# Retention and two mixtures of experts on one core: the front's work moved between engines

## The chip, the core and the metric

The kernel runs on one core of a Trainium2 chip. The metric is device time in microseconds (us). A core has a matrix engine (TensorE, PE in rows; its weight loads are PEld), VectorE (DVE), ScalarE (ACT), GpSimd (POOL) and SyncE (SP), which here only issues transfers. Each engine works through its own list of instructions in order and waits on semaphores for the others.

## The reference

All arithmetic is in 32-bit floats. With 2 sequences, 8 heads, 768 steps and head size 64:

```
state = gamma * state + k_t (x) v_t         per head, 64 x 64
y_t   = q_t . state / sqrt(64)              -> x, 1536 tokens x 512
logits = x @ w_gate  (8 experts)            expert = argmax, weight = softmax at it
each token goes to its expert, in order, up to capacity 384
h = relu(x @ w1[e]); y = h @ w2[e]          8 experts, hidden size 1024
out = sum over 4 domains of p_d * (relu(y @ u1[d]) @ u2[d])
```

## The kernel before

The program has a front (retention, routing, gathering the first expert's tokens) and then two long matrix stages, the 8 experts and the 4 domain experts. The change touches the front alone.

The front takes the 1536 tokens in 12 tiles of 128 steps (6 to a sequence) and is a software pipeline, written out by hand in the loop of line 458: `tc.manual_schedule()` keeps the written order on every engine. Round `it` works on several tiles at once:

- `st_v` (247): v of tile it+1 times a decay per head, on GpSimd, into vg.
- `st_S` (257): scores k.q of tile it for 8 heads, on TensorE, 64 rows by 128 columns at a time; then VectorE multiplies by the causal mask into sd.
- `st_I`, `st_U`, `st_O` (301, 278, 315): state times q, update of the state sum, and vg times sd, all for tile it-1 on TensorE. ScalarE copies the state out (st). The sixth tile of a sequence has no U, the first no I.
- `st_x` (327): the output of tile it-1 times a scale table gqs. ScalarE copies it out of the accumulation memory (PSUM) to ot, GpSimd multiplies into xT; for the last two tiles VectorE does both in one step.
- `x_pe` and `x_reduce` (355, 374), tile it-2: TensorE multiplies xT by iw, an identity beside the gate's weights, which turns the tile back and yields the logits. VectorE sums the logits, ScalarE copies the tokens to xk, and ScalarE's queue stores xk to memory.
- `x_dve` (393), tile it-2: eight small steps on VectorE to the one-hot expert choice ohs, the running count cum and ohk, the one-hot times the token's number.
- `r_pe` and `r_dve` (347, 420), tile it-3: a rank of each token in its expert from two small products, read back by VectorE, and compared with slot numbers (`slot_at`, at).
- `g_pe` (443), tile it-4: at times ohk sums up which token sits in which slot.

`braid` (451) emits two chains of VectorE step by step in turn. The kernel uses eight banks of PSUM: four rotate among scores, outputs, ranks and warm-up; four are held for the slots, the state, and X (x0 and x1).

SyncE issues loads in a fixed order: qk and kv of a tile (512 KB each), the tables gqs (256 KB each), iw and kc. Round `it` loads tile it+3. From round 6 on the first weights are loaded as well, and at the end of round 8 `split_w(0)` (131) splits one: a copy on ScalarE, then a subtraction on VectorE.

After the loop (500 to 581) the last tiles run out. `late` multiplies tokens of the last two tiles straight into the first expert's input T0x; `fetched` adds those that a GpSimd gather brought from memory. Line 950 is the first expert product.

Of the kernel before, what the change touches and what calls it, by code (L numbers as in the profile page):

```python
# [29 lines left out]
XW = KD * 136  # L30
# [5 lines left out]
DEPTH = 4  # L36
HT = 384
# [21 lines left out]
def tile_retention_moe_moe(ctx: ExitStack, tc, qkv, cst, gqt, a0, a1, a2, b1, b2, out, cap):  # L59
# [16 lines left out]
    banks = [f"bank{n}" for n in range(4)]  # L76
    held = ["slot", "u", "x0", "x1"]
    nbank = [0]

    def bank(name, tag=None):  # L80
        if tag is None:
            tag = banks[nbank[0] % len(banks)]
            nbank[0] += 1
        return ps[0].tile([P, 512], F32, tag=tag, name=name)

# [107 lines left out]
    with ExitStack() as actx:  # L193
# [7 lines left out]
        iw = pa.tile([P, KD, 136], F32, name="iw")  # L201
        zero = pa.tile([1, D], F32, name="zero")
# [7 lines left out]
        slot_ps = bank("slot_ps", "slot")[:, 0:SL // P * E1].rearrange(  # L210
# [21 lines left out]
        load_qk(1)  # L232
        load_gq(0)
        load_kv(1)
        nc.sync.dma_start(out=iw.rearrange("p a b -> p (a b)"), in_=cst[:, C_IW:C_U])
        load_qk(2)
        nc.sync.dma_start(out=kc, in_=cst[:, C_U:])
        load_gq(1)
        load_kv(2)
# [7 lines left out]
        def st_v(i):  # L247
            kv = kv_t.pop(i)
            vg = p2.tile([P, 8, HD], F32, tag="vg", name=f"vg{i}", bufs=3)
            nc.gpsimd.tensor_tensor(  # L250
                out=vg, in0=kv[:, 1].rearrange("p (h d) -> p h d", h=8),
                in1=gk[:, i % NCH].rearrange("p (h d) -> p h d", d=1).to_broadcast([P, 8, HD]),
                op=ALU.mult,
            )
            live[i] = {"vg": vg, "k": kv[:, 0]}

        def st_S(i):
            qk = qk_t.pop(i)
            sd = p2.tile([P, 2, 512], F32, tag="sd", name=f"sd{i}")
            live[i].update(sd=sd, q=qk[:, 0])  # L260
            bks = [bank(f"S{i}_{j}") for j in range(2)]
            for hp in range(4):
                cols = slice(hp * P, (hp + 1) * P)
                for j in range(2):
                    r = slice(64 * j, 64 * j + 64)
                    nc.tensor.matmul(
                        out=bks[j][:, cols], lhsT=qk[r, 1, cols], rhs=qk[r, 0, cols],
                        start=True, stop=True,
                    )
# [8 lines left out]
        def st_U(i):  # L278
# [3 lines left out]
            if c == 0:  # L282
                u_ps[0] = bank(f"U{i}", "u")
# [17 lines left out]
        def st_I(i):  # L301
            c = i % NCH
            live[i]["o"] = [bank(f"O{i}_{j}") for j in range(2)]
# [23 lines left out]
        def st_x(i):  # L327
# [4 lines left out]
            if i < NT - 2:  # L332
                ot = p2.tile([P, 512], F32, tag="ot", name=f"ot{i}")
                for j in range(2):
                    nc.scalar.copy(ot[:, 256 * j:256 * j + 256], bks[j][:, 0:256])
                nc.gpsimd.tensor_tensor(out=xT, in0=ot, in1=gqs[:, c], op=ALU.mult)
            else:
                for j in range(2):
                    cols = slice(256 * j, 256 * j + 256)
                    nc.vector.tensor_tensor(  # L340
                        out=xT[:, cols], in0=bks[j][:, 0:256], in1=gqs[:, c, cols], op=ALU.mult
                    )
# [4 lines left out]
        def r_pe(i):  # L347
            bk = bank(f"R{i}")
            nc.tensor.matmul(out=bk[:, 0:8], lhsT=onesb, rhs=cum[:, i], start=True, stop=False)
            nc.tensor.matmul(out=bk[:, 0:8], lhsT=ub, rhs=ohs[:, i], start=False, stop=True)  # L350
            rl[i] = bk[:, 0:8]

        xks = {}

        def x_pe(i, reduce=True):
            xT = live.pop(i)["xT"]
            xk = xks[i] = p2.tile([P, D], F32, tag="xk", name=f"xk{i}", bufs=3)
            part = p2.tile([P, 8], F32, tag="part", name=f"part{i}")
            if i == NT - 1:
                bks = [bank(f"X{i}_{g}") for g in range(2)]  # L360
            else:
                bks = [bank(f"X{i}_{g}", f"x{g}") for g in range(2)]
            for hp in range(KD):
                nc.tensor.matmul(
                    out=bks[hp // 2][:, (hp % 2) * 136:(hp % 2 + 1) * 136],
                    lhsT=xT[:, hp * P:(hp + 1) * P], rhs=iw[:, hp], start=True, stop=True,
                )
            xbs[i] = bks, part
# [3 lines left out]
        xbs = {}  # L372

        def x_reduce(i):
            bks, part = xbs.pop(i)
            xk = xks[i]
            for g in range(2):
                b3 = bks[g][:, 0:272].rearrange("p (q c) -> p q c", q=2)
                nc.vector.tensor_reduce(
                    out=part if g else lgs[:, i], in_=b3[:, :, P:136].rearrange("p q e -> p e q"),  # L380
                    axis=AX.X, op=ALU.add,
                )
                nc.scalar.copy(
                    xk.rearrange("p (b k c) -> p k b c", b=4, k=KD)[:, 2 * g:2 * g + 2],
                    b3[:, :, 0:P].rearrange("p q (b c) -> p q b c", b=4),
                )
            nc.scalar.dma_start(out=xd[1 + i * P:1 + (i + 1) * P], in_=xk)
            nc.vector.tensor_tensor_reduce(
                out=lgs[:, i], in0=lgs[:, i], in1=part, scale=1.0, scalar=-FMAX, op0=ALU.add,
                op1=ALU.max, accum_out=mxs[:, i],  # L390
            )
# [161 lines left out]
        for b in range(SL // P):  # L553
            fetched(b, range(2))
# [858 lines left out]
```

## Time and profile before

| | |
|---|---|
| median of 3 runs | 735.69 us (735.53 to 737.09) |
| profiled execution | 735.49 us |
| its span, first to last instruction | 733.7 us |
| granted TensorE clock | 0.999 |
| PE busy | 722.3 us (98%) |
| DVE, ACT, POOL busy | 473.5, 339.0, 202.5 us |

Times in rows count from the start of the span. A row of the timeline has its start, its duration, the engine, the line, the operation, what is written and read, and, in brackets, the idle time just before it with what ended it. Rows of one line that follow one another are merged, with their count. Each 32-bit product shows as two passes (16 for the 8 score products). A row of a stretch has the length, then busy time and instructions of PE, PEld, DVE, ACT and POOL, the granted clock, the share of the DMA engines and GB/s.

### The profile page before, as it was taken

How to read it: one execution, taken by the hardware profiler on the slowest of the kernel's cores; microseconds unless marked ns; L12 is line 12 of the kernel's file. 1: busy time of each engine (PE TensorE's matmuls, PEld its weight loads, DVE VectorE, ACT ScalarE, POOL GpSimd, SP SyncE). 2: the span in 40 equal slices, each digit the busy share in tenths (PEclk: the TensorE clock that was granted, in tenths of full speed). 3: DMA queues.
4: the chain of work that ended last, by engine and by line, in shares of the span. 5: the costliest groups of instructions: out<-in, count | busy, mean ns of one | idle time of the engine just before them, and what ended most of it. 6: DMA issues, size and time to landing. Idle time of an engine off the chain costs nothing.

```text
span 733.7 us, 11338 instructions
## 1 busy us (share of the span) xinstructions
PE 722.3 (98%) x4425; PEld 657.2 (90%) x4426; DVE 473.5 (65%) x777; ACT 339.0 (46%) x545; POOL 202.5 (28%) x193
## 2 busy tenths in 40 slices
PE   8998999999999999999999999999999999999997
PEld 6887999999999888999889998889998899988896
DVE  3888899898898835545743655763475454557334
ACT  2344767676656533334433445633344334444331
POOL 3653854443044012212323111223422121111103
PEclk9999999999999999999999999999999999999999
DMA  9984886687741211211122122122222212112102
GB/s 331 414 338 138 287 320 220 228 281 245 230 144 34 89 55 59 86 58 58 61 91 78 38 77 87 59 85 88 87 72 71 92 53 86 59 58 79 37 1 86
DMA packets 28026, 92.83 MB, mean 127 GB/s; under 512 B 4097, under 2 KB 4369, under 8 KB 27970
## 3 DMA queue, kind: packets, MB, share of 16 engines
q1 hardware_dynamic: 23042, 81.79, 32.2%
q0 software_dynamic: 3056, 7.05, 2.8%
q10 hardware_dynamic: 1872, 3.24, 1.2%
q8 instruction: 35, 0.57, 0.3%
q14 instruction: 21, 0.17, 0.1%
HBM read 85.72 MB, written 6.34 MB: 125 GB/s over the span
## 4 chain that ended last, share of the span: by engine, by line
PE 88%; DVE 1%; POOL 1%; ACT 0%; issue 0%; POOLq 0%; ACTq 0%
PE o L1212 35%; PE a L1056 17%; PE m L950 15%; PE b L1056 9%; PE m L953 7%; PE bb L1056 5%; POOL out_dram L1224 1%; PE ab L1056 0%; DVE x L855 0%; DVE X L868 0%; ACT X L864 0%; DVE c L1149 0%; POOLq L1409 0%; ACT c L1087 0%; PE T L768 0%
## 5 line engine op out<-in xcount | busy, mean ns | idle before, releaser
L1212 PE MATMUL o<-w,g_c 128*128 128x512 f32 x1152 | 267.4, 390 | 0.0
L1212 PEld LDWEIGHTS o<-w,g_c 128*128 128x128 f32 x1152 | 215.9, 188 | 43.7
L142 DVE TENSOR_TENSOR w<-raw,w 128x1024 fp32r<-128x1024 f32 x128 | 158.4, 1247 | 13.9 <-ACT w L141 13.6
L1056 PE MATMUL a<-X,w 128*128 128x384 f32 x720 | 145.2, 336 | 0.0
L157 POOL TENSOR_TENSOR t<-raw 128x512 f32<-128x512 f32 x28 | 38.8, 1386 | 349.6 <-DMA raw<-b 302.2
L1091 DVE TENSOR_TENSOR c<-b,c 128x384 f32<-128x384 f32 x30 | 16.7, 558 | 181.1 <-PE b L1056 181.1
L141 ACT CAST w<-raw 128x1024 fp32r<-128x1024 f32 x128 | 132.1, 1047 | 2.5 <-DMA raw<-a 1.1
L1056 PEld LDWEIGHTS a<-X,w 128*128 128x128 f32 x720 | 127.5, 188 | 2.6 <-DVE c L1091 0.3
L1087 ACT COPY c<-a 128x384 f32<-128x384 f32 x60 | 28.8, 479 | 196.3 <-PE a L1056 196.3
L950 PE MATMUL m<-xet,w 128*128 128x448 f32 x256 | 80.8, 375 | 0.8 <-PEq L635 0.8
L1072 ACT ACTIVATE g_c<-c 128x384 fp32r<-128x384 f32 x96 | 50.4, 526 | 66.0 <-DVE c L1091 64.7
L950 PE MATMUL m<-h,w 128*128 128x448 f32 x256 | 80.8, 375 | 0.0
L1056 PE MATMUL b<-X,w 128*128 128x384 f32 x360 | 72.1, 334 | 0.0
L953 PE MATMUL m<-h,w 128*128 128x224 f32 x256 | 67.5, 264 | 0.0
L953 PE MATMUL m<-xet,w 128*128 128x224 f32 x256 | 67.5, 264 | 0.0
L624 POOL DMA_INDIRECT xe<-xd,gidx x42 | 53.7, 1278 | 47.3 <-DVE xT L752 35.7
L1056 PEld LDWEIGHTS b<-X,w 128*128 128x128 f32 x360 | 63.5, 188 | 0.0
L1076 DVE SCALAR_TENSOR_TENSOR g_c<-c,g_c 128x384 fp32r<-128x384 f32 x96 | 52.9, 552 | 3.9
L950 PEld LDWEIGHTS m<-xet,w 128*128 128x128 f32 x256 | 48.0, 187 | 4.6 <-PEq L635 1.0
L950 PEld LDWEIGHTS m<-h,w 128*128 128x128 f32 x256 | 48.0, 187 | 3.7
L953 PEld LDWEIGHTS m<-xet,w 128*128 128x128 f32 x256 | 48.9, 191 | 0.0
L953 PEld LDWEIGHTS m<-h,w 128*128 128x128 f32 x256 | 48.9, 191 | 0.0
(158 smaller groups left out, 766.7 us busy)
## 6 DMA issues: line engine op xcount, KB each, us to landing
raw<-a SPq DMA_DIRECT2D x64, 512.0 KB, 4.9
raw<-b SPq DMA_DIRECT2D x64, 512.0 KB, 3.5
qk<-qkv SPq DMA_DIRECT2D x12, 512.0 KB, 8.3
kv<-qkv SPq DMA_DIRECT2D x12, 512.0 KB, 8.1
xd<-xk ACTq DMA_DIRECT2D x12, 256.0 KB, 6.2
gqs<-gqt SPq DMA_DIRECT2D x6, 256.0 KB, 7.5
xe<-xd,gidx POOLq DMA_INDIRECT x44, 4.9
iw<-cst SPq DMA_DIRECT2D x1, 272.0 KB
```

Source lines behind the costliest of these rows:

```text
L141: nc.scalar.copy(w[:, 0], r)
L142: nc.vector.tensor_tensor(out=w[:, 1], in0=r, in1=w[:, 0].bitcast(F32), op=ALU.subtract)
L157: eng.tensor_tensor(out=c[:, 0:2], in0=b[:, 2:4], in1=b[:, 1:3], op=sub)
L624: nc.gpsimd.indirect_dma_start(out=t[:, b], out_offset=None, in_=xq, in_offset=bass.IndirectOffsetOnAxis(ap=gidx[:, b, e:e + 1], axis=0),)
L950: nc.tensor.matmul(out=b2, lhsT=w[0], rhs=x, start=first, stop=last, skip_group_check=True)
L953: nc.tensor.matmul(out=b2[:, 0], lhsT=w[1], rhs=x[:, 0], start=False, stop=last, skip_group_check=True)
L1056: nc.tensor.matmul(out=bk[:, 0:HT], lhsT=w[:, sw, k], rhs=x[:, sx, k], start=(first and m == 0), stop=(m == len(steps) - 1), skip_group_ch ...
L1072: nc.scalar.activation(out=h2[:, 0], in_=src, func=AF.Relu)
L1076: nc.vector.scalar_tensor_tensor(out=h2[:, 1], in0=src, scalar=0.0, in1=h2[:, 0].bitcast(F32), op0=ALU.max, op1=ALU.subtract,)
L1087: nc.scalar.copy(t, bk[:, 0:HT])
L1091: nc.vector.tensor_tensor(out=t, in0=bk[:, 0:HT], in1=t, op=ALU.add)
L1212: nc.tensor.matmul(out=bk, lhsT=h2[:, sh, cols], rhs=w[:, sw, k], start=(q == 0 and m == 0 and (n, t) not in begun), stop=(m == 2), skip_g ...
```

## The change

- v (from tile 2 on) is made on ScalarE, one instruction for each of the 8 heads.
- The output product is always made by VectorE straight from PSUM; the copy to ot and GpSimd's product go.
- A score product is cut into two of 64 rows by 64 columns, and from round 4 on the scores of tile it are issued at the start of round it.
- PSUM: one bank pair each for scores (s2), outputs (o2) and X (x), besides slot and u. The rank product goes into X's second bank, ahead of X. One reduction takes all four logit parts, one copy makes xk, and the maximum is a plain reduction.
- ohk moves to ScalarE; the slot numbers get a 16-bit copy, rnk16, for the comparison.
- iw is loaded as one identity and the gate's weights (ig, 80 KB instead of 272 KB) and spread by ScalarE in round 1.
- Loads: kv of tiles 1 and 2 go ahead of the tables.
- The end runs in another order.

```
-        load_gq(0)
         load_kv(1)
-        nc.sync.dma_start(out=iw..., in_=cst[:, C_IW:C_U])
+        load_gq(0)
         load_qk(2)
+        load_kv(2)
+        nc.sync.dma_start(out=ig, in_=cst[:, C_IW:C_U])
         nc.sync.dma_start(out=kc, in_=cst[:, C_U:])
         load_gq(1)
-        load_kv(2)
...
 def st_v(i):
+            if i < 2:
                 nc.gpsimd.tensor_tensor(out=vg, in0=v, in1=..., op=ALU.mult)
+            else:
+                for h in range(8):
+                    nc.scalar.activation(
+                        out=vg[:, h], in_=v[:, h], func=AF.Copy, scale=gk[:, i % NCH, h:h + 1]
+                    )
...
 def st_S(i):
-            bks = [bank(f"S{i}_{j}") for j in range(2)]
+            s2 = two("s2", f"S{i}")
+            bks = [s2[:, j] for j in range(2)]
             for hp in range(4):
-                for j in range(2):
+                for m in range(4):
+                    o, j = 64 * (m >> 1), m & 1
                     nc.tensor.matmul(
-                        out=bks[j][:, cols], lhsT=qk[r, 1, cols], rhs=qk[r, 0, cols],
+                        out=bks[j][o:o + 64, cols],
+                        lhsT=qk[r, 1, hp * P + o:hp * P + o + 64], rhs=qk[r, 0, cols],
...
 def st_x(i):
-            if i < NT - 2:
-                    nc.scalar.copy(ot[:, 256 * j:256 * j + 256], bks[j][:, 0:256])
-                nc.gpsimd.tensor_tensor(out=xT, in0=ot, in1=gqs[:, c], op=ALU.mult)
-            else:
                 for j in range(2):
                     nc.vector.tensor_tensor(out=xT[:, cols], in0=bks[j][:, 0:256], ...)
...
+        def x_pe(i, rank=None, reduce=True):
+            b2 = xbs[i] = two("s2" if i == NT - 1 else "x", f"X{i}")
+            if rank is not None:
+                r_pe(rank, b2[:, 1, 448:456])
...
 def x_reduce(i):
+            nc.vector.tensor_reduce(out=lgs[:, i], in_=b3[:, :, P:136]..., axis=AX.X, op=ALU.add)
+            nc.scalar.copy(xk..., b3[:, :, 0:P]...)
             nc.scalar.dma_start(out=xd[1 + i * P:1 + (i + 1) * P], in_=xk)
+            nc.vector.tensor_reduce(out=mxs[:, i], in_=lgs[:, i], axis=AX.X, op=ALU.max)
...
         for it in range(NT):
+            if it >= EARLY_S:        # 4
+                st_S(it)
             ...
-            st_S(it)
+            if it < EARLY_S:
+                st_S(it)
...
         st_I(NT - 1)
-        x_pe(NT - 2)
-        r_pe(NT - 3)
         st_O(NT - 1)
-        braid(r_dve(NT - 3))
-        g_pe(NT - 4)
-        g_pe(NT - 3)
         st_x(NT - 1)
+        x_pe(NT - 2, NE - 1, False)
+        g_pe(NE - 2)
+        braid(r_dve(NE - 1))
+        g_pe(NE - 1)
         (slot numbers out, gather issued)
+        x_reduce(NT - 2)
+        x_pe(NT - 1, None, False)
         braid(x_dve(NT - 2))
-        x_pe(NT - 1, False)
-        r_pe(NT - 2)
-        braid(r_dve(NT - 2))
+        r_pe(NT - 2, one("u", "R10")[:, 0:8])
         x_reduce(NT - 1)
-        braid(x_dve(NT - 1))
+        braid(r_dve(NT - 2), x_dve(NT - 1))
```

## Rows read from the trace of the kernel before

**Rows 1.** Busy time by stretches: the rounds, the end, the expert stages.
```profile
20.00:55.00 35.00, 34.58 (x569) 30.44 (x569) 29.81 (x115) 12.96 (x38) 20.23 (x22) 1.00 0.93 374
55.00:68.40 13.40, 11.11 (x112) 9.66 (x111) 10.73 (x59) 4.26 (x10) 2.12 (x2) 1.00 0.41 134
68.40:733.70 665.30, 659.42 (x3528) 604.43 (x3528) 424.07 (x583) 316.67 (x484) 173.44 (x158) 1.00 0.32 107
```

**Rows 2.** Timeline of the weight loads, one round.
```profile
48.96 0.97 PEld L266 LDWEIGHTS S<-qk 64*128 64x128 f32 x16 [0.17 <-issue]
50.05 0.99 PEld L364 LDWEIGHTS X<-iw,xT 128*128 128x128 f32 x8
...
51.26 0.43 PEld L309 LDWEIGHTS O<-qk,st 64*64 64x64 f32 x16
51.86 0.55 PEld L290 LDWEIGHTS U<-vg,kv 128*64 128x64 f32 x16 [0.17 <-issue]
52.32 0.91 PEld L321 LDWEIGHTS O<-sd,vg 128*64 128x64 f32 x16
53.40 0.30 PEld L266 LDWEIGHTS S<-qk 64*128 64x128 f32 x4 [0.17 <-issue]
```

**Rows 3.** The same timeline: X of tiles 1, 2 and 9, and one wait.
```profile
18.79 0.99 PEld L364 LDWEIGHTS X<-iw,xT 128*128 128x128 f32 x8
...
23.32 0.99 PEld L364 LDWEIGHTS X<-iw,xT 128*128 128x128 f32 x8
...
35.30 0.96 PEld L266 LDWEIGHTS S<-qk 64*128 64x128 f32 x14 [0.54 <-DVE ranks L424]
...
54.49 0.99 PEld L364 LDWEIGHTS X<-iw,xT 128*128 128x128 f32 x8
```

**Rows 4.** Timeline of GpSimd: v of tiles 3 and 4.
```profile
19.59 1.04 POOL L250 TENSOR_TENSOR vg<-kv,cdec 128x512 f32<-128x512 f32 x1 [2.26 <-PE X L364]
...
22.93 1.04 POOL L250 TENSOR_TENSOR vg<-kv,cdec 128x512 f32<-128x512 f32 x1 [1.06 <-DMA kv<-qkv]
```

**Rows 5.** ScalarE: first xk (timeline); groups (count, busy us, mean ns, idle before).
```profile
17.53 0.65 ACT L383 COPY xk<-X 128x256 f32<-128x256 f32 x2 [4.21 <-DVE lgs L379]
...
L383 ACT COPY xk<-X 128x256 f32<-128x256 f32 x24 | 7.8, 375 | 21.2 <-DVE lgs L379 18.1 <-DVE part L379 3.1
L141 ACT CAST w<-raw 128x1024 fp32r<-128x1024 f32 x6 | 6.2, 1048 | 1.3 <-DMA kv<-qkv 0.9 <-ACT xk L383 0.4
```

**Rows 6.** DMA issues: size of iw.
```profile
iw<-cst SPq DMA_DIRECT2D x1, 272.0 KB
```

**Rows 7.** Timeline of VectorE in the last round.
```profile
53.52 0.76 DVE L340 TENSOR_TENSOR xT<-O,gqs 128x256 f32<-128x256 f32 x2
54.59 1.29 DVE L271 TENSOR_TENSOR sd<-S,cdec 128x512 f32<-128x512 f32 x2 [0.31 <-PE S L266]
55.80 0.17 DVE L379 TENSOR_REDUCE lgs<-X 128x8 f32<-128x16 f32 x1
...
56.44 0.16 DVE L424 CUSTOM_DVE_ANT_0 sel<-R,ohs 128x8 f32<-128x8 f32 x1
...
56.91 0.23 DVE L401 TENSOR_SCALAR ohs<-cd,cm 128x8 f16<-128x8 f32 x1
...
57.25 0.22 DVE L412 TENSOR_SCALAR ohk<-ohs,kc 128x8 f16<-128x8 f16 x1
```

**Rows 8.** Timeline of VectorE: its part of the first weight split.
```profile
44.95 1.23 DVE L142 TENSOR_TENSOR w<-raw,w 128x1024 fp32r<-128x1024 f32 x1 [0.79 <-ACT w L141]
```

**Rows 9.** Weight loads of the end: last X, last late product, first expert product.
```profile
59.25 0.99 PEld L364 LDWEIGHTS X<-iw,xT 128*128 128x128 f32 x8 [0.43 <-DVE xT L340]
...
63.48 1.43 PEld L528 LDWEIGHTS T0x<-at,xk 128*128 128x128 f32 x8 [0.61 <-ACT w L141]
...
68.42 0.19 PEld L950 LDWEIGHTS m<-xet,w 128*128 128x128 f32 x1 [0.96 <-PEq L635]
```

More of the change, by code (lines that the diff above doesn't have):

```diff
@@ L75, in tile_retention_moe_moe, with two, one, bank @@
     ps = [sctx.enter_context(tc.tile_pool(name="ps", bufs=1, space=PSUM))]
-    banks = [f"bank{n}" for n in range(4)]
-    held = ["slot", "u", "x0", "x1"]
+    pairs = ["s2", "o2"]
     nbank = [0]
[L80 to L83, printed above, removed]
+    def two(tag, name):
+        return ps[0].tile([P, 2, 512], F32, tag=tag, name=name)
+    def one(tag, name):
         return ps[0].tile([P, 512], F32, tag=tag, name=name)
+    def bank(name):
+        nbank[0] += 1
+        return two(pairs[nbank[0] % 2], name)[:, 0]
     def warm(n, fill):
@@ L302, in st_I @@
             c = i % NCH
-            live[i]["o"] = [bank(f"O{i}_{j}") for j in range(2)]
+            o2 = two("o2", f"O{i}")
+            live[i]["o"] = [o2[:, j] for j in range(2)]
             q = live[i].pop("q")
@@ L343, in st_x, with r_pe @@
             d["xT"] = xT
         rl = {}
[L347 to L351, printed above, removed]
+        def r_pe(i, bk):
+            nc.tensor.matmul(
+                out=bk, lhsT=onesb, rhs=cum[:, i], start=True, stop=False, skip_group_check=True
+            )
+            nc.tensor.matmul(
+                out=bk, lhsT=ub, rhs=ohs[:, i], start=False, stop=True, skip_group_check=True
+            )
+            rl[i] = bk
@@ L353, in tile_retention_moe_moe @@
         xks = {}
-        def x_pe(i, reduce=True):
+        xbs = {}
+        def x_pe(i, rank=None, reduce=True):
             xT = live.pop(i)["xT"]
[L357 to L362, printed above, removed]
+            xks[i] = p2.tile([P, D], F32, tag="xk", name=f"xk{i}", bufs=3)
+            b2 = xbs[i] = two("s2" if i == NT - 1 else "x", f"X{i}")
+            if rank is not None:
+                r_pe(rank, b2[:, 1, 448:456])
@@ L376, in x_reduce @@
             xk = xks[i]
[L377 to L386, printed above, removed]
+            b3 = xbs.pop(i).rearrange("p g (q c) -> p (g q) c", q=2)
@@ L549, in tile_retention_moe_moe @@
         slot_at(NT - 1)
-        late(NE + 1)
+        late(NT - 1, range(KD))
         g_pe(NT - 2)
         g_pe(NT - 1)
-        for b in range(SL // P):
-            fetched(b, range(2))
+        fetched(k01)
         nc.vector.tensor_scalar(
@@ L572, in tile_retention_moe_moe @@
         nc.vector.tensor_copy(rows, slot_ps.rearrange("p b e -> p (b e)"))
-        rps = bank("rows", "u")[:, 0:NB4 * E1]
+        rps = one("u", "rows")[:, 0:NB4 * E1]
         for b in range(NB4):
@@ L579, in tile_retention_moe_moe @@
             )
-        for b in range(SL // P):
-            fetched(b, range(2, KD))
+        fetched(k23)
     def offsets():
```

134 lines of the change are left out of this document (72 added, 62 removed).

## The prediction

> **What bounds the kernel now.** I read the busy time by stretches first. From 20 to 55 us TensorE is busy 34.58 of 35.00 us, VectorE 29.81, GpSimd 20.23, ScalarE 12.96, and the DMA engines are at 0.93. From 55 to 68.4 us TensorE is busy 11.11 of 13.40 us. After 68.4 us it is busy 659.42 of 665.30 us and the change touches nothing there [rows 1]. So whatever moves the first expert product, at 68.42 [rows 9], moves the end by the same amount, and only the front counts.
>
> The weight loads of TensorE in time order then show one round of the front. Scores start at 48.96, the token product X at 50.05, the state product I at 51.26, U at 51.86, O at 52.32, and the next scores at 53.40: 4.44 us, with 0.17 us idle ahead of U and of the scores [rows 2]. I call X of token tile n X(n). X(1) starts at 18.79, X(2) at 23.32, X(9) at 54.49 [rows 3]. From X(2) to X(9) are 31.17 us. Seven rounds of 4.44, less one U (0.46) and one I (0.60) that tiles 5 and 6 don't have [rows 2], are 30.02, so 1.15 us there are waits, the largest a 0.54 us wait of the scores for a rank [rows 3].
>
> Third are the loads: GpSimd's product for v starts when a kv tile has landed, at 19.59 and 22.93 for tiles 3 and 4 [rows 4]. (The releaser printed at 19.59 is a matmul that has no part in v, so I take that time too as the landing.) Here the queue is full: 374 GB/s at a DMA share of 0.93 [rows 1].
>
> **The change part by part.** The sum is made on the profiled execution, 735.49 us (span 733.7 and 1.8 around it), 0.2 us under the median of the runs, 735.69.
>
> *Scores on quarters.* A round's 16 passes of 64x128 become 32 of 64x64. That is the form of I, whose 16 passes take 0.43 us [rows 2]: 0.86 for 32. The scores now take 50.05 - 48.96 = 1.09, so a round gets shorter by 0.23, to 4.21. Bounds: a gain of 0.23, or a loss of 0.85 if each new pass takes what a 64x128 pass takes now (0.97/16 = 0.061). I take the gain, since the row has the same shape. The rank product moves from its own bank to just before X in X's bank: same instructions, nothing in TensorE's time.
>
> *v on ScalarE.* Eight activations of 64 columns take the place of one GpSimd product, from tile 2 on. ScalarE takes 1.048 us for 1024 columns and 0.375 for 256, which is 0.876 ns a column, so 0.21 for 64; two copies in a row take 0.65, 0.10 less than twice one [rows 5]. Eight: 1.0 (8 x 0.11 and the last one's tail); bounds 0.9 and 1.7 (no overlap). I take 1.0. In ScalarE's queue they stand ahead of the copy xk of the round, of the store of xk, and of the new ohk, which is also ScalarE's now. TensorE cannot start the next X before xk is copied out: X has one pair of banks. The single xk copy of 512 columns is 0.375 + 256 x 0.876 ns = 0.60.
>
> So X(1) has to wait for the landing of kv tile 3, its v, and xk(0). The constant iw shrinks from 272 KB [rows 6] to 80 KB, 0.5 us at 374 GB/s, so kv tile 3 lands at 19.1. 19.1 + 1.0 + 0.6 + 0.1 for the handovers = 20.8, and the rank product 0.1: X(1) at 20.9 instead of 18.79. What was hidden behind GpSimd is on the path. Then X(2): kv tile 4 at 22.4, v and xk(1) until 24.1, and the rank read on VectorE stands behind xk(1) (next paragraph); from it to the end of ohs are 57.14 - 56.44 = 0.7 [rows 7], then the rank product: X(2) at 25.0 to 25.2. TensorE alone gives 20.9 + 4.2 = 25.1. I take 25.2, which is 1.9 later than before. The copies that build iw (0.6 and 0.2) and the output products of the first tiles, which now wait for later tables, move X(0) to about 15; X(1)'s wait covers all of it. Without that cover they would cost 1.1. Later kv tiles land over 1 us before they are needed.
>
> *Output and the token chain on VectorE.* Added: two products of 256 columns, 0.76 a round. Gone: one of two reductions, ohk, and the lock-ups with GpSimd. Undisturbed, VectorE's chain from the logits to ohk takes 57.25 - 55.80 = 1.45 without ohk, the score products 1.29 [rows 7]. Rank and tokens now share a bank pair. Before, xk always starts behind VectorE's reduction of the same bank: 4.21 us idle at 17.53, 21.2 us over all [rows 5], though neither needs the other's data. Two engines that read one bank go one after the other here. So the rank read, which now follows xk in the order of that tile, stands behind its 0.6: the chain becomes 1.9. With 1.29 and 0.76 VectorE needs 3.95 of 4.21 us a round. The comparison against a rank row of 16 bits instead of 32 is not in the trace; the whole stretch from the rank read to ohs, which holds it, is 0.47 [rows 7], so it can save between nothing and that; I take nothing.
>
> The Trainium skill (PSUM — Partial Sum Buffer, section PSUM bank collisions raise a hardware error) asks that accesses of two engines to one bank be kept apart, reads against reads included. The trace agrees (the 21.2 us of idle). By that rule the chain is 1.9 and the time the one I forecast; were the rank read free of it, the chain would be 1.45 and the time some 0.6 lower.
>
> *One bank pair for the scores.* Scores used four rotating banks; now they have one pair, so scores of tile n+1 wait until VectorE has read those of tile n. In an even round there is 0.6 us of room. At X(2) VectorE is late from xk(1): 24.2 + 0.8 + 1.29 + 0.1 = 26.4 against scores at 25.2 + 1.07 = 26.3, so 0.2 with the handover. In round 8 the first weight is split: ScalarE 1.05 [rows 5], then VectorE 1.23, which waited 0.79 for ScalarE [rows 8]. Both stand ahead of the score product. From X(6): logits + 1.3, ohs and ohk + 2.1, ScalarE's part + 1.05, VectorE's + 1.23, score product + 1.29: 6.97. TensorE wants the bank at 4.21 + 1.07 = 5.28. Wait: 1.7 (bounds 0 and 2.6). In the kernel before the four banks hide this.
>
> *Other end order.* Before: the last X at 59.25, 4.76 after X(9), and the last late product at 63.48, 8.99 after it [rows 9]. After: X(9), slot product, I, O, X(10), slot products and the rank's comparison put the last X at 4.6; then two chains of VectorE are braided and I reach the last late product at 9.1. I take + 0.1; bounds - 1.0 (the 0.43 and 0.61 waits of these rows both gone) and + 1.1 (X(10) with its rank now stands behind O, and nothing hides it). The gather's issue, on GpSimd, stands behind the slot product as before and some 0.2 earlier.
>
> *Sum.* X(2): + 1.9. From X(2) to X(9): 7 x 4.21 - 1.06 + 0.2 + 1.7 = 30.3 against 31.17: - 0.9. End: + 0.1. Together + 1.1: 736.6 us.
>
> **Rivals.** *VectorE becomes the bound of the loop* (the other side). It has 3.95 of 4.21 us; from 0.26 more a round it sets the pace. For it: its chain hands over to ScalarE and back in every round, and eight activations may be in the way. Against it: GpSimd's lock-ups end. At 4.45 a round, 7 x 0.24 = 1.7 more: 738.3, slower.
>
> *One of the two waits does not come.* Without the bank wait (VectorE quicker on 16-bit rows, no rank behind xk): 736.6 - 1.9 = 734.7. Without the wait for kv tiles at the start, also 736.6 - 1.9 = 734.7. For it: both are worked out, neither is seen. Against it: single bank pairs and the order of ScalarE's queue stand in the code.
>
> *Neither comes*: 732.8. It needs kv tile 3 two us earlier than its bytes say.
>
> *The quarters do not run abreast*, so that the change does not do what it says: 1.08 a round over seven rounds, 744.2. Against it stands I, the same shape at 0.43.
>
> **How the numbers follow.** The forecast has 0.43, VectorE as the bound 0.28, one wait missing 0.16, neither 0.10, quarters 0.03. A measurement of this kernel can tell about 0.2%, 1.5 us, from no change: 734.2 to 737.2. My case is 735.7 to 737.6 by its own bounds (0.3 of it on the slow side), VectorE's lies almost all above, one wait missing mostly inside, neither below. That gives faster 0.14, same 0.46, slower 0.40. The range runs from 734.2 to 738.8: it leaves out the last two cases (0.13) and a fifth of VectorE's.
>
> **What would show it.** Right: weight loads of the scores at about 0.86 for 32, a round of 4.2; X(1) near 20.9 behind v and xk on ScalarE; a wait of the scores for VectorE near the first weight split, between 47 and 50 us; the first expert product at 69.5. Wrong: X(1) before 19.5, no wait of the scores, or score loads over 1.1 us.

## The result and the profile after

The changed kernel takes 741.42 us in the median of 5 runs (740.42 to 743.81), the kernel before 735.63 us beside it: 1.0083 times as long, 95% interval 1.0068 to 1.0097. I had said 736.6 and at most 738.8. The profiled execution takes 741.42 us, its span is 739.7 us, 6.0 more than before. (In the series of e1, of e5_three and of e10 the kernel before took about 740 us itself, and one chip gave 740.35 beside e10 and 736.63 beside e12, so ratios are compared inside a series only.)

The front came out near the forecast. Weight loads of the changed kernel in time order (start, duration, tile, operands, count, and the idle time before with what ended it):

```profile
18.70 0.86 PEld L281 LDWEIGHTS S<-qk 64*64 64x64 f32 x32 [0.17 <-issue]
...
20.67 0.99 PEld L377 LDWEIGHTS X<-iw,xT 128*128 128x128 f32 x8
...
47.48 0.89 PEld L281 LDWEIGHTS S<-qk 64*64 64x64 f32 x32 [0.80 <-PE X L377]
...
54.78 0.99 PEld L377 LDWEIGHTS X<-iw,xT 128*128 128x128 f32 x8
...
59.48 0.99 PEld L377 LDWEIGHTS X<-iw,xT 128*128 128x128 f32 x8
...
62.09 0.68 PEld L519 LDWEIGHTS T0x<-at,xk 128*128 128x128 f32 x4 [1.48 <-ACT xk L392]
...
63.95 1.43 PEld L519 LDWEIGHTS T0x<-at,xk 128*128 128x128 f32 x8 [0.27 <-ACT w L145]
...
67.00 0.52 PEld L528 LDWEIGHTS T0x<-ident,xe 128*128 128x128 f32 x4 [0.83 <-DMA xe<-xd,gidx]
...
67.68 0.97 PEld L528 LDWEIGHTS T0x<-ident,xe 128*128 128x128 f32 x8
71.37 0.29 PEld L965 LDWEIGHTS m<-xet,w 128*128 128x128 f32 x1 [2.72 <-issue]
```

The 32 score passes take 0.86 [rows 2: 0.97 for 16 wide ones]. X(1) starts at 20.67, X(9) at 54.78, 0.29 behind [rows 3], where the sum had 1.0. The last late product is at 63.95, 9.17 after X(9), where I had reached 9.1. Up to there the kernel has lost 0.47 us against [rows 9]. Then it falls behind: from that row to the first expert product it needs 7.42 us, where [rows 9] need 4.94.

ScalarE and VectorE of the changed kernel show where. The xet rows turn the first expert's input into the parts that the products read: ScalarE rounds half a T0x, VectorE takes the remainder.

```profile
18.10 2.02 ACT L265 ACTIVATE vg<-kv,cdec 128x64 f32<-128x64 f32 x8 [2.45 <-DMA kv<-qkv]
20.03 0.56 ACT L392 COPY xk<-X 128x512 f32<-128x512 f32 x1
...
68.85 0.53 ACT L798 CAST xet<-T0x 128x448 fp32r<-128x448 f32 x1 [5.21 <-PE T0x L528]
...
71.28 0.53 ACT L798 CAST xet<-T0x 128x448 fp32r<-128x448 f32 x1 [1.90 <-DVE xet L802]
```

```profile
44.98 1.23 DVE L146 TENSOR_TENSOR w<-raw,w 128x1024 fp32r<-128x1024 f32 x1 [1.11 <-ACT w L145]
46.13 1.28 DVE L287 TENSOR_TENSOR sd<-S,cdec 128x512 f32<-128x512 f32 x2
...
56.85 0.17 DVE L430 CUSTOM_DVE_ANT_0 sel<-X,ohs 128x8 f32<-128x8 f32 x1 [0.20 <-ACT xk L392]
...
59.68 0.16 DVE L541 CAST gidx<-slot_ps 128x2 int32<-128x2 f32 x1 [0.30 <-PE slot_ps L452]
...
66.17 0.17 DVE L588 CAST rows<-slot_ps 128x16 f16<-128x16 f32 x1
70.63 0.62 DVE L802 TENSOR_TENSOR xet<-T0x,xet 128x448 fp32r<-128x448 f32 x1 [4.29 <-issue]
```

```profile
60.71 1.15 POOL L544 DMA_INDIRECT xe<-xd,gidx  x1 [46.78 <-ACT xk L392]
```

Three things are late in the 2.48 us. GpSimd starts the gather at 60.71, 0.87 after the slot numbers of 59.68 are written (at 59.84), and the gathered rows hold TensorE up for 0.83; that puts the last eight products at 67.68, 0.72 further from the late product than before. ScalarE's first half starts at 68.85, when *all* of T0x is there. And VectorE's first half starts at 70.63, 1.25 after ScalarE's ended at 69.38, while no row shows what it waits for; ScalarE's second half waits for it in turn.

Around TensorE's gap of 2.72 us the clock is low as well, and that costs a second time. Busy time by stretches (length, then PE, PEld, DVE, ACT, POOL, the granted clock, DMA share, GB/s) of the changed kernel:

```profile
20.00:55.00 35.00, 33.42 (x706) 29.93 (x705) 27.72 (x106) 26.20 (x92) 0.00 (x0) 1.00 0.92 366
55.00:71.37 16.37, 11.34 (x112) 9.82 (x112) 9.46 (x49) 4.15 (x9) 3.52 (x4) 0.96 0.37 117
...
70.00:75.00 5.00, 3.60 (x12) 3.37 (x13) 3.63 (x12) 2.42 (x3) 2.83 (x4) 0.50 0.38 110
75.00:80.00 5.00, 5.00 (x29) 4.71 (x28) 3.41 (x4) 2.71 (x5) 3.78 (x5) 0.82 0.82 251
71.37:739.70 668.33, 662.33 (x3528) 606.80 (x3528) 422.19 (x583) 317.33 (x485) 173.93 (x157) 1.00 0.32 106
```

From 70 to 75 us the granted clock is 0.50, the lower of the two levels (1.2 GHz), where [rows 1] have 1.00 in the mean; until it rises the first expert's products go at half speed. The same turning products that stand 10.04 us behind the first expert product before stand 12.55 behind it here (71.37 to 83.92): 2.5 us more. With the 2.95 at 71.37 this makes 5.46 of the 6.0; the other 0.5 is not located.

### The profile page after: what moved, and what is told of

Its sections match the earlier page's. It is cut to its first block, busy times and chain, and to the rows that moved or that the text cites. A ratio compares the mean times of both kernels' runs of the same rounds, so it can differ in the third digit from the quotient of the medians.

```text
span 739.7 us, 11724 instructions
## 1 busy us (share of the span) xinstructions
PE 722.4 (98%) x4617; PEld 657.3 (89%) x4618; DVE 467.4 (63%) x762; ACT 354.3 (48%) x607; POOL 181.4 (25%) x173
## 4 chain that ended last, share of the span: by engine, by line
PE 93%; DMA 3%; DVE 1%; ACT 1%; issue 1%; POOL 1%; SPq 0%; POOLq 0%; ACTq 0%
PE o L1227 35%; PE a L1071 17%; PE m L965 15%; PE b L1071 8%; PE m L968 7%; PE bb L1071 5%; PE X L377 1%; PE S L281 1%; PE O L338 1%; DMA kv<-qkv 1%; DMA gqs<-gqt 1%; DMA xe<-xd,gidx 1%; PE U L306 1%; POOL out_dram L1239 1%; PE O L326 0%
## 5 line engine op out<-in xcount | busy, mean ns | idle before, releaser
L146 DVE TENSOR_TENSOR w<-raw,w 128x1024 fp32r<-128x1024 f32 x128 | 156.3, 1231 | 15.4 <-ACT w L145 15.3
L965 PE MATMUL m<-xet,w 128*128 128x448 f32 x256 | 83.3, 383 | 2.6 <-DVE xet L802 2.6
L965 PEld LDWEIGHTS m<-xet,w 128*128 128x128 f32 x256 | 49.3, 193 | 6.7 <-issue 2.7
L968 PEld LDWEIGHTS m<-xet,w 128*128 128x128 f32 x256 | 50.1, 196 | 0.0
```

Of the source, the lines that this page charges most:

```text
L146: nc.vector.tensor_tensor(out=w[:, 1], in0=r, in1=w[:, 0].bitcast(F32), op=ALU.subtract)
L965: nc.tensor.matmul(out=b2, lhsT=w[0], rhs=x, start=first, stop=last, skip_group_check=True)
L968: nc.tensor.matmul(out=b2[:, 0], lhsT=w[1], rhs=x[:, 0], start=False, stop=last, skip_group_check=True)
```

## Experiments

### Each late step by itself

My theory: three independent things make the end late: the buffer that the gather fills, T0x as one tile over two banks, and the place of VectorE's two pieces in its list of instructions. The rival: it is the order of the end. e1 gives the gather's target another buffer, e2 makes T0x two tiles, e3 puts 11 small writes early in VectorE's list, so that all that follows stands further back, e4 puts the end back into the order of before.

```
 # e1
-xe0 = pq.tile([P, SL // P, D], F32, tag="kv", name="xe0")
+xe0 = pq.tile([P, SL // P, D], F32, tag="qk", name="xe0")
 # e2
-x2p = two("x", "T0x")
-xt0 = [x2p[:, g, 0:2 * SM]... for g in range(2)]
+x2p = [two("x", "T0x0"), two("o2", "T0x1")]
+xt0 = [x2p[g][:, 0, 0:2 * SM]... for g in range(2)]
+pairs[1] = "s2"
 # e3
+for _ in range(11):
+    nc.vector.memset(small[:, 0:1], 0.0)
 # e4
 st_I(NT - 1)
+x_pe(NT - 2, NE - 1)
 st_O(NT - 1)
+braid(r_dve(NE - 1))
+g_pe(NE - 2)
+g_pe(NE - 1)
 st_x(NT - 1)
-x_pe(NT - 2, NE - 1, False)
-g_pe(NE - 2)
-braid(r_dve(NE - 1))
-g_pe(NE - 1)
...
-x_reduce(NT - 2)
+braid(x_dve(NT - 2))
 x_pe(NT - 1, None, False)
-braid(x_dve(NT - 2))
 r_pe(NT - 2, one("u", "R10")[:, 0:8])
+braid(r_dve(NT - 2))
 x_reduce(NT - 1)
-braid(r_dve(NT - 2), x_dve(NT - 1))
+braid(x_dve(NT - 1))
```

> The changed kernel with one edit: the gather of the first expert's tokens lands in a buffer that qk tiles used instead of kv tiles, so that GpSimd no longer waits for ScalarE as well before it. Theory: the gather started 0.87 us after its slot numbers (59.84 to 60.71) where the kernel before took 0.29, because the wait for VectorE came in an instruction ahead of the gather and the gather's own start-up is no longer hidden behind it. Then the first gather starts 0.2 to 0.4 us after the slot numbers, TensorE's wait for the gathered rows falls from 0.83 to about 0.3, and the first expert product comes 0.4 to 0.6 us earlier than 71.37. Rival: GpSimd starts slowly because it was idle for 47 us; then nothing moves (0.8 to 0.9 us as before). Time: 740.8 by the theory if the clock still drops, 738 if it does not; 741.4 by the rival.

> The changed kernel with one edit: the first expert's input T0x stands in two PSUM tiles (the first banks of the X pair and of the output pair) instead of both banks of one tile. Theory: in one tile every reader waits for all of its products, so ScalarE's first copy now starts at about 67.8, when the products of the first half end, instead of 68.85, and its second copy no longer waits for VectorE's subtraction. If VectorE is late at 70.63 only because of that copy, its subtraction comes at 68.4 and the first expert product at 69.3 to 69.6 (time 738 to 739 with less or no half clock). Rival: VectorE's 3.4 us after its branch are a fetch of instructions; then its subtraction stays at 70.4 to 70.7, the first product at 71.2 to 71.4, and the time at 741.

> The changed kernel with eleven one-column VectorE memsets added at the start, where VectorE is idle, so that its branch stands at the same place in its list of instructions as in the kernel before. Theory: after the branch VectorE has to fetch instructions from memory (3.4 us from the branch at 67.19 to the subtraction at 70.63; at most 0.75 us in the kernel before), and whether it must depends on where the branch stands; then the subtraction follows ScalarE's copy at about 69.4, the first expert product comes at 70.1 to 70.3 instead of 71.37, and the time falls by 1.2 us or, with a shorter half clock, up to 3 us: 738 to 740. Rival: VectorE waits for something else; then nothing moves, 741.4.

> The changed kernel with the end in the order of the kernel before (X of tile 10 with its reduction ahead of the last outputs, one token chain after the other), on the new banks. Forecast's reading: the order of the end is worth 0.1 us (741.3). If instead the new order is what costs the end, the last late product comes earlier than 63.95 by 0.3 to 0.5 and the time falls by as much or, through the clock, by up to 3 us. Rival: the new order was a gain that something else ate; then the last late product comes 0.5 us or more later than 63.95 and the time is 742.

Measured: e1 743.81 us, 1.0037 [1.0022, 1.0053] times the kernel before of the series; e2 743.16, 1.0034 [1.0017, 1.0051]; e3 741.76, 1.0016 [0.9998, 1.0035]; e4 744.1, 1.0049 [1.0036, 1.0063]. The mechanisms show in the rows, first e1's gather, on VectorE and GpSimd:

```profile
60.65 0.16 DVE L541 CAST gidx<-slot_ps 128x2 int32<-128x2 f32 x1 [0.30 <-PE slot_ps L452]
```

```profile
61.10 1.15 POOL L544 DMA_INDIRECT xe<-xd,gidx  x1 [46.85 <-DVE mxs L397]
```

It starts 0.29 after the slot numbers instead of 0.87. In e2 the second half of ScalarE's work follows TensorE and no longer VectorE:

```profile
68.48 0.53 ACT L799 CAST xet<-T0x 128x448 fp32r<-128x448 f32 x1 [4.42 <-PE T0x L528]
69.61 0.53 ACT L799 CAST xet<-T0x 128x448 fp32r<-128x448 f32 x1 [0.59 <-PE T0x L528]
```

In e3 VectorE starts 0.03 after ScalarE's end (69.64) instead of 1.25, and the first expert product comes at 70.41:

```profile
69.67 0.62 DVE L804 TENSOR_TENSOR xet<-T0x,xet 128x448 fp32r<-128x448 f32 x1 [3.00 <-ACT xet L800]
```

```profile
70.41 0.19 PEld L967 LDWEIGHTS m<-xet,w 128*128 128x128 f32 x1 [1.51 <-issue]
```

So each is there and each goes with its own edit; in e1 and e2 the others remain and the first expert product is at 73.20 and 72.41. In three profiles of the changed kernel as it is that product comes at 71.37, 71.91 and 73.30, so what e1 and e2 are worth there by themselves can't be read; in e1 TensorE's clock is 0.78 from 60 to 65 us, and it never waits for the gathered rows. The old order (e4) brings nothing: the last late product comes 9.84 after X(9) instead of 9.17, the first expert product is at 72.07, and the time can't be told from e1's. Why the order of the list matters to VectorE is inferred: 11 writes that nothing waits for remove the wait, so it is the place in the list and not the work; that the instructions themselves arrive late is the likely reason, and no row shows it.

### All three, and two things more

after_again is the changed kernel once more, e5_three has e1 to e3 together. e6_early_v adds v on GpSimd for tiles 2 to 4 as well, against the 2.02 us of ScalarE in front of X(1). e7_fill adds warm-up products to e6 in the two gaps before the first expert product, against the lower clock.

```
 # e6
-            if i < 2:
+            if i < 5:
                 nc.gpsimd.tensor_tensor(out=vg, ...)
 # e7
+        warm(3, fill)      # ahead of the first gathered rows
...
+        warm(8, fill)      # behind the second
```

> The changed kernel once more, beside the kernel before on the chip of the experiments, so that the experiments can be compared with it. If the experiments' chip treats both kernels alike, the ratio is that of the first comparison, 1.008 (1.0068 to 1.0097). If the loss lies in the two places that the trace shows at 60 to 72 us (the gather late, VectorE's products for the first expert late) and in the lower clock behind them, the first expert product comes at 71 to 73 and a stretch of TensorE at 1.2 GHz follows within 2 us of it.

> The gather into qk's buffers, the first expert's tokens in two tiles and 11 small memsets ahead in VectorE's list, together. Theory (the three causes at the end add up and the lower clock follows from the idle time of TensorE that they make): the gather starts 0.3 us after its slot numbers, the copies for the first expert follow the first half of its tokens, VectorE follows ScalarE at once: the first expert product 2.5 to 3 us earlier than in the changed kernel, at 68.5 to 70, no stretch at 1.2 GHz in most runs, and a time 4 to 6 us under the changed kernel on the same chip: ratio to the kernel before 0.999 to 1.003. Rival (the clock falls whatever these do): the first expert product earlier by as much, the lower clock still there, ratio 1.004 or more.

> As the run with the three edits, and v of tiles 0 to 4 on GpSimd again (later ones on ScalarE). Theory (the copy of X(0) and of X(1) stood behind v's eight activations): X(1) comes one round of TensorE after X(0), at 19.6 to 20 instead of 20.7, X(2) at 23.8 to 24.2 instead of 24.9, and everything after it 0.8 to 1.0 us earlier than in the run with three edits: ratio 0.998 to 1.001. Rival (the loads or VectorE decide by then, and the gain is given back as a wait later): X(2) earlier, X(9) not, no difference to the run with three edits.

> As the run with early v on GpSimd, and 11 matmuls of 512 columns of zeros (3 before the gathered rows are brought in, 8 between them and the first expert product) while TensorE has nothing to do. Theory (the lower clock follows from the idle time of TensorE at 60 to 70 us): no stretch at 1.2 GHz in any run, the times of the runs lie within 1 us of one another instead of 3 to 4, and the median is 0.5 to 1.5 us below the run without them. Rival (the lower clock has another cause): the spread of the runs stays, and the fillers cost up to 1 us.

Measured, against the kernel before: after_again 743.45 us, 1.0037 [1.0024, 1.0051]; e5_three 742.9, 1.0037 [1.0023, 1.0050]; e6 742.83, 1.0036 [1.0023, 1.0048]; e7 743.41, 1.0044 [1.0032, 1.0057]. e5 has its first expert product at 70.15, 3.15 earlier than after_again (73.30), and its time is only 0.55 lower: my theory of a fixed distance to the end fails. Part of the 3.15 is the clock: from 60 to 65 us it is 0.77 in after_again and 1.00 in e5. In e6 X(1) is at 19.82, 0.85 earlier than in the changed kernel, but X(9) at 56.04, later: the scores wait 1.09 at 21.90 and 1.18 at 48.74, the output product 1.06 at 37.33, and what was gained is gone, as the rival has it. In e7 the clock is 1.00 in all stretches from 60 to 75 us, but so it is in e6's profile, which makes e7 no test of the clock; its runs spread over 2.2 us (e6's over 1.8), the fillers stand in front of the first expert product (71.56) and the time doesn't fall.

### Where the gain goes

On a chip where the kernel before takes 736.3 us the changed kernel, e5 and e6 ran once more, beside the kernel before (before_third; before_again is a single run of it).

> The kernel before, profiled on the chip of the experiments, where its median is 740.4 us against 735.63 in the first comparison at a granted clock that is as high. If the front takes longer there, X(9) and the first expert product come 4 us or more later than the 54.49 and 68.42 of the first profile. If the expert stage takes longer there, the first expert product comes within 1.5 us of 68.42 and waits of TensorE of 2 to 4 us stand between 78 and 95 us, as in the other profiles of this chip, and the lag of the weight loads behind the first profile grows there and not later.

> The changed kernel once more, beside the two repeated experiments, all on one chip. Theory (the end of the front decides: gather late, VectorE late, TensorE's lower clock behind them): 1.005 to 1.010 of the kernel before, the first expert product at 71 to 73. Rival (a wait that comes later, at 78 to 92 us, sets the time whatever the front does): the lag behind the kernel before grows between 78 and 92 us.

> The three edits of the end together, a second time. Theory: the first expert product 2 to 3 us earlier than in the changed kernel on this chip, no stretch at 1.2 GHz in most runs, and 3 us or more less: ratio to the kernel before 0.999 to 1.003. Rival (a wait at 78 to 92 us takes it back): first expert product as early, but the lag behind the kernel before grows by 2 to 5 us between 78 and 92 us, and the ratio is that of the changed kernel.

> The three edits and v of tiles 0 to 4 on GpSimd, a second time. Theory: X(1) at 19.5 to 20, and 0 to 1 us below the run with three edits, since VectorE's turn around the first weight split gives most of it back: X(8) within 1 us of the run with three edits.

> The kernel before as a run of its own, for its profile on the same chip as the three others: ratio 0.998 to 1.002. If waits of 2 to 5 us stand between 78 and 92 us in its profile too, they belong to the chip; if they stand only in the changed kernels, they belong to the change.

before_third: 736.19 us, 1.0002 [0.9993, 1.0011]; before_again 737.06. after_third: 743.36, 1.0095 [1.0080, 1.0109]; e5_second 742.06, 1.0076 [1.0064, 1.0088]; e6_second 742.28, 1.0084 [1.0071, 1.0097]. I follow three places in the weight loads: the first expert product, and the product on h that the next expert's input releases. The kernel before, the changed one, and e5:

```profile
68.31 0.19 PEld L950 LDWEIGHTS m<-xet,w 128*128 128x128 f32 x1 [0.97 <-PEq L635]
...
84.43 0.19 PEld L950 LDWEIGHTS m<-h,w 128*128 128x128 f32 x1 [0.22 <-DVE xet L775]
```

```profile
71.91 0.29 PEld L965 LDWEIGHTS m<-xet,w 128*128 128x128 f32 x1 [2.30 <-issue]
...
92.02 0.19 PEld L965 LDWEIGHTS m<-h,w 128*128 128x128 f32 x1 [1.84 <-DVE xet L790]
```

```profile
69.70 0.29 PEld L968 LDWEIGHTS m<-xet,w 128*128 128x128 f32 x1 [1.44 <-DVE xet L805]
...
84.59 0.19 PEld L968 LDWEIGHTS m<-h,w 128*128 128x128 f32 x1 [1.16 <-issue]
90.18 0.19 PEld L968 LDWEIGHTS m<-h,w 128*128 128x128 f32 x1 [1.84 <-DVE xet L793]
```

The changed kernel is 3.60 behind at the first row, 5.91 at the turning products (84.25 against 78.34), 7.59 at the second row, and 7.0 in the span. e5 is 1.39 behind at the first row, 2.97 at the turning products (a clock of 0.69 from 70 to 75 us), 5.75 at its last row (90.18), and 5.2 in the span. Of the 2.21 by which e5 is ahead of the changed kernel at the first row it still has 1.84 at the last; what it does not win back is 2.78 between the turning products and the last row, in two waits of TensorE, at 84.59 and 90.18. e6 has no low clock until the first of these waits (1.00 from 65 to 80 us; 0.66 from 85 to 90, behind its wait of 2.00 at 84.83), is 2.37 behind at its first row and 6.00 at its last. The low stretch of e5:

```profile
70.00:75.00 5.00, 5.00 (x23) 4.68 (x23) 3.18 (x7) 1.79 (x4) 3.78 (x5) 0.69 0.67 193
```

Behind these waits stands ScalarE. Its timeline, the kernel before and e5:

```profile
76.43 0.53 ACT L977 COPY tsum<-m 128x448 f32<-128x448 f32 x1 [0.47 <-DVE h L980]
```

```profile
77.95 1.05 ACT L145 CAST w<-raw 128x1024 fp32r<-128x1024 f32 x1
82.18 0.53 ACT L995 COPY tsum<-m 128x448 f32<-128x448 f32 x1 [3.17 <-PE m L971]
```

TensorE's last pass of the group that these copies read, in the kernel before and in e5:

```profile
75.83 0.26 PE L953 MATMUL m<-xet,w 128*128 128x224 f32 x1
```

```profile
78.80 0.26 PE L971 MATMUL m<-xet,w 128*128 128x224 f32 x1
```

So ScalarE starts 0.34 after that pass ends in the kernel before (and waits for VectorE there, so it may have known earlier), and 3.12 after it in e5; the weights' casts and the next expert's input, which stand behind the copy on ScalarE and then VectorE, are late by as much, and TensorE, which has 0.22 us to spare there before, waits. By the rows alone the product is done and nobody has been told. The Trainium skill (Perfetto Trace Analysis, section Tensor Engine Instruction (MATMUL, LD_WEIGHTS)) says that a recorded end of TensorE is an estimate, and that the semaphore moves only when the accumulation memory has confirmed the writes. e5's row names that product as the releaser, 3.12 us after its recorded end, so the recorded end can be that far from the signal. What delays it stays open.

### Scores on quarters alone; scores on halves again

e8_quarters_alone is the kernel *before* with only the score products cut into quarters. e9_three_halves is e5 with halves. Two questions: is the quarter a gain by itself, and do the late signals come from its 192 additional instructions on TensorE?

```
 # e8, in the kernel before
-                for j in range(2):
+                for m in range(4):
+                    o, j = 64 * (m >> 1), m & 1
...
-                        out=bks[j][:, cols], lhsT=qk[r, 1, cols], rhs=qk[r, 0, cols],
+                        out=bks[j][o:o + 64, cols],
+                        lhsT=qk[r, 1, hp * P + o:hp * P + o + 64], rhs=qk[r, 0, cols],
 # e9: the same lines the other way round, in e5
```

> The kernel before with one part of the change alone: the scores on quarters of the array (32 passes of 64x64 instead of 16 of 64x128). Theory of the prediction (TensorE's time gets shorter by 0.23 us a round and nothing else is touched): first expert product 1.5 to 2.3 us earlier than 68.4, at 66.1 to 67, ratio 0.997 to 0.999. Rival (the loads, at a DMA share of 0.93, hold the rounds at 4.44 us): ratio 0.999 to 1.001. Rival for the waits at 80 to 92 us (they come with the 192 more instructions in TensorE's list and the other places at which it is fetched): such a wait of 1.5 to 3 us stands here too, and the ratio is 1.001 to 1.004.

> The three edits of the end, with the scores on halves of the array again, so that TensorE's list is as long as in the kernel before. Theory (quarters give 0.23 us a round): the first expert product 1 to 2.5 us later than in the run with three edits, at 70.7 to 72.2, ratio 1.008 to 1.012. If the waits of 1.5 to 3.6 us at 80 to 92 us come with the length of TensorE's list, they are gone and the ratio is 1.004 to 1.007 all the same; if they come with the other parts of the change, they stay.

e8 takes 736.06 us, 0.9994 [0.9985, 1.0003]: no change, though the first expert product is at 67.77, 0.54 earlier than in before_third. e9 takes 743.63, 1.0092 [1.0078, 1.0105]. Weight loads of e8, then of e9:

```profile
52.94 0.86 PEld L267 LDWEIGHTS S<-qk 64*64 64x64 f32 x32 [0.17 <-issue]
53.98 0.99 PEld L366 LDWEIGHTS X<-iw,xT 128*128 128x128 f32 x8 [0.17 <-issue]
...
67.77 0.19 PEld L952 LDWEIGHTS m<-xet,w 128*128 128x128 f32 x1 [0.95 <-PEq L637]
```

```profile
87.26 0.19 PEld L966 LDWEIGHTS m<-h,w 128*128 128x128 f32 x1 [2.13 <-issue]
...
92.86 0.19 PEld L966 LDWEIGHTS m<-h,w 128*128 128x128 f32 x1 [1.85 <-DVE xet L791]
```

In e8 the passes cost 0.86 as in the changed kernel, but X then waits 0.17 behind them, so scores and handover take 1.04 instead of 1.09: only 0.05 of the 0.23 us a round arrives. In the changed order, where the scores stand at the start of the round, they are worth nearly all of it: e9's round with halves takes 4.43 us (X at 52.75 and 57.18), the changed kernel's 4.22 (50.56 and 54.78), and e9's X(9) comes 2.29 later than e5_second's (54.89). The late waits are in e9 without the additional instructions and not in e8 with them, so they neither suffice nor are needed.

### Loads, output and v by themselves

e10_quarters_loads adds to e8 the small iw, spread by ScalarE, and the early kv loads; e11_quarters_xT_dve adds to e8 the output of every tile on VectorE; e12_three_v_gpsimd is e5 with v of every tile on GpSimd.

```
 # e10, in e8
-        load_gq(0)
         load_kv(1)
-        nc.sync.dma_start(out=iw..., in_=cst[:, C_IW:C_U])
+        load_gq(0)
         load_qk(2)
+        load_kv(2)
+        nc.sync.dma_start(out=ig, in_=cst[:, C_IW:C_U])
...
+            if it == 1:
+                nc.scalar.copy(iw[:, :, 0:P], eye)
+                nc.scalar.copy(iw[:, :, P:136], ig[:, P:XW]...)
 # e11, in e8
-            if i < NT - 2:
+            if i < 0:
 # e12, in e5
-            if i < 2:
+            if i < NT:
```

> The quarters and the loads of the change on the kernel before: the constant iw is loaded as 80 KB instead of 272 and spread by two ScalarE copies, and kv tiles 1 and 2 are asked for ahead of the constants; v stays on GpSimd, the output as before. Theory (the first X wait for kv tiles): the 1.35 us wait of U for v at 16.57 shrinks by 0.5 to 1.0, X(1) to X(11) and the first expert product come as much earlier, at 66.8 to 67.3, ratio 0.997 to 0.999. Rival (the two copies on ScalarE delay X(0), and the waits only move): first expert product at 67.5 or later, ratio 0.999 to 1.001.

> The quarters and the output product of every tile on VectorE, on the kernel before (v stays on GpSimd, the banks, the reductions and the end order as before). Theory (VectorE has 0.76 us a round more and is no bound as long as the two reductions stay under 4.4 us): first expert product within 0.7 us of the run with quarters alone, no waits at 80 to 92 us, ratio 0.998 to 1.001. Rival (VectorE with both reductions and the output is the bound): rounds of 4.5 us or more, first expert product at 69 or later, ratio 1.002 to 1.006.

> The three edits of the end, and v of every tile on GpSimd again. Theory (v on ScalarE, 2 us a tile ahead of the copy xk, is what keeps the front behind): X(1) at 19.5 to 20, X(9) at 53.5 to 54.5, first expert product at 68 to 69.2, ratio 0.999 to 1.003. Rival (the banks and VectorE's list decide: the scores wait for VectorE in any case): X(9) at 55 to 56 as in the run with early v on GpSimd, first expert product at 70 to 71, ratio 1.006 to 1.009.

e10 takes 740.99 us, 1.0011 [0.9993, 1.0029]; e11 742.11, 1.0027 [1.0008, 1.0046]; e12 742.71, 1.0079 [1.0066, 1.0093]. In e10 X(1) comes 0.60 earlier than in e8 (18.54), and the first expert product is at 69.18 all the same: the output product waits 1.61 later on, for VectorE's score product. In e11 it is VectorE's part of the weight split that stands in front of the score product (the row of 1.05 names no releaser). The waits of e10, with VectorE's rows ahead of the score product, and of e11:

```profile
38.89 0.42 PEld L312 LDWEIGHTS O<-qk,st 64*64 64x64 f32 x14 [1.61 <-DVE sd L274]
```

```profile
36.05 1.19 DVE L412 TENSOR_TENSOR cum<-cum,ohs 128x8 f16<-128x8 f16 x1
37.16 1.08 DVE L415 TENSOR_SCALAR ohk<-ohs,kc 128x8 f16<-128x8 f16 x1
```

```profile
46.65 0.10 PEld L352 LDWEIGHTS <-ub 128*128 128x128 f16 x1 [1.05 <-issue]
...
47.58 0.42 PEld L311 LDWEIGHTS O<-qk,st 64*64 64x64 f32 x14 [0.35 <-DVE sd L273]
```

The two steps of e10 take 0.16 and 0.22 us one round later. Here they end at 37.24 and 38.24, and two products of GpSimd (at 35.95 and 37.18, of 1.26 and 1.04) at 37.21 and 38.22; that GpSimd holds them up is read from these times.

e11's forecast of no wait at 80 to 92 us fails. TensorE waits 1.63 at 86.50 there and 1.59 at 86.68 in e10, behind a late copy on ScalarE as in e5. e10's weight load, the copy, and the last pass of the group that it reads:

```profile
86.68 0.19 PEld L957 LDWEIGHTS m<-h,w 128*128 128x128 f32 x1 [1.59 <-DVE xet L782]
```

```profile
81.05 0.53 ACT L984 COPY tsum<-m 128x448 f32<-128x448 f32 x1 [2.02 <-PE T L775]
```

```profile
79.21 0.27 PE L960 MATMUL m<-xet,w 128*128 128x224 f32 x1
```

The copy starts 1.57 after the recorded end of that pass, and its row names a product of TensorE as the releaser. Neither e10 nor e11 has the change's banks, its end or v on ScalarE, and e8, which they build on, has no such wait; but e8 ran in another series, and in that of e10 and e11 the kernel before took 740.35 us itself and was not profiled.

In e12 X(1) starts at 19.42 without ScalarE's 2.02 us, and X(9) at 55.18, 0.40 *later* than in the changed kernel; the scores wait 1.09 at 21.50 and 1.33 at 47.88, until 0.07 and 0.08 after the end of VectorE's score products (at 20.15 and 46.52, of 1.28). So v on ScalarE isn't what holds the front back. That one bank pair and VectorE's list give the pace, as the rival has it, fits these rows; no run took the pair away.

## Why the prediction was wrong

- *Scores on quarters*: right. 0.86 for 32 as said. The two quarters of a product run side by side, and the rival at 744.2 is out, though the time came near it for another reason.
- *v on ScalarE*: the mechanism was right and the term too small. Eight activations take 2.02 us, 0.25 each, where I took 1.0 and bounded at 1.7. kv of tile 3 was there by 18.10, a microsecond before my 19.1, and the two errors nearly cancel: X(1) at 20.67 for 20.9, X(2) at 24.85 for 25.2. That these times came out is luck.
- *Rank behind xk*: right. VectorE's rank read at 56.85 is released by ScalarE's xk. That is what the rule of the Trainium skill (PSUM — Partial Sum Buffer, section PSUM bank collisions raise a hardware error) gave; the trace agrees. It is a semaphore of the program that ends this wait, and no run shows the two reads without it.
- *VectorE as the bound of the loop*: rejected. The round from 50.56 to 54.78 takes 4.22 us for the forecast 4.21, and VectorE is busy 27.72 of 35.00 us, less than in [rows 1].
- *One bank pair for the scores*: the wait is there, at 47.48, right behind VectorE's part of the first weight split (44.98, after 1.11 for ScalarE), and takes 0.80 instead of 1.7. VectorE's score product ends at 47.41, 0.07 before the scores start. Their row names X as the releaser, so that it is VectorE's read that ends it is my reading of the order, not the row's.
- *Other end order, + 0.1*: the first step that failed. I followed the end to the last late product and took what lies behind it, 4.94 us [rows 9], as untouched, because the code there is hardly changed. It takes 7.42. Its work is the same; what changed is what the work depends on: a buffer's earlier user, the size of the tile that readers wait for, and a place in the list of instructions. e1 to e3 show each of the three, and together they bring the first expert product forward by 3.15 us (e5_three against after_again, part of it the clock) and 2.21 (e5_second against after_third). Why the place in the list matters is not shown.
- *"Whatever moves the first expert product moves the end by the same amount"*: the second failure. In the profiled runs 2.95 at that product became 6.0 at the end, 2.5 of it a stretch at the lower clock; [rows 1] show the stages behind as full, and I read that as a fixed length. It isn't: from the first expert product to the end of the span are 665.3 us before and 668.3 in the changed kernel, and beside one another 666.0 in before_third, 669.4 in after_third and 669.8 in e5_second. With e5 the product comes 2.21 us earlier than in after_third and the span is 1.8 shorter (the median time 1.3); against the kernel before the waits at 84.59 and 90.18 cost it 2.78, where the kernel before waits 0.22.

What is open: why ScalarE hears of TensorE's products up to 3 us late. The number of TensorE's instructions (e8, e9), v on ScalarE (e12, which waits 1.83 at 85.30) and the low clock (e6_second has none before its late signals) are not needed for it. The chip of e5_second does not make it by itself: before_third ran there and has no such wait. The change's banks and end are not needed either, since e10 and e11 show it without them, in a series in which the kernel before was slow too. Whether the change, the series or both bring it was not told apart. So of e5's 5.2 us of span against before_third, 1.39 stand at the first expert product and 1.58 in the lower clock; the 2.78 that follow (2.97 to 5.75) are located but have no shown cause, and some 0.5 come back later. Nothing that I ran beats the kernel before; e8 equals it, and the intervals of e3 and e10 hold 1 as well, in series in which the kernel before took 740 us.

## What to carry to other kernels

A change of buffers, banks or places in an engine's list can be paid for in code that the diff doesn't touch, so the chain has to be followed to the point where the engine is full again and not to the last edited line. A stage in which the engine is busy 99% still has waits that stand a fraction of a microsecond from being late, and a delay ahead of it can grow there: ask for the slack of its first transfers and casts. Time won early in a tight loop can be given back at its next wait; e6, e10 and e12 each won 0.6 to 1.3 us at X(1) and lost it.

## What the hardware showed

- One activation of 64 columns with a scale per partition costs 0.25 us even in a row of eight (2.02 us); ScalarE's 512 columns in one copy cost 0.56.
- VectorE can start 1.25 us late with nothing to wait for in the profile, and 11 small writes early in its list remove it (e3).
- Around TensorE's wait of 2.72 us that ended at 71.37 the granted clock was 0.50 from 70 to 75 us, and the products up to the turning ones took 2.5 us longer. With a wait of 1.44 there it was 0.69 in e5_second and 1.00 in e6_second: that wait alone doesn't decide. Without any low clock from 60 to 85 us (e5_three) the time was 742.9 all the same.
- A GpSimd gather starts 0.29 or 0.87 us after its indices, by the buffer it writes (e1).
- A signal of TensorE reached ScalarE 3.12 us after the recorded end of the product in e5 and 1.57 in e10, at most 0.34 in the kernel before.
- Two steps of 8 columns on VectorE took 1.19 and 1.08 us instead of 0.16 and 0.22, and each ended within 0.03 us of a product on GpSimd (e10).
